# Fetching two weight matrices in turn, and a new order of the first units' decays, splits and masks, in a gated-attention and ELU-MLP kernel

## The chip, the cores and the metric

The kernel runs on one core of a Trainium2 chip. The metric is the device time of one execution in microseconds (us), lower is better. The work is done by five engines with queues of their own: TensorE (PE in the profile, PEld for its weight loads), VectorE (DVE), ScalarE (ACT), GpSimd (POOL) and SyncE (SP), which only issues DMAs here.

## The reference

Two stages follow each other. The first is a gated linear recurrence for 4 batches, 8 heads, 768 tokens and a head size of 48. The second is an MLP with an ELU, on 3072 tokens.

```python
f = 1.0 / (1.0 + np.exp(-f_logit))
for t in range(S):
    state = f[:, :, t, :, None] * state + np.einsum('bhd,bhe->bhde', k[:, :, t], v[:, :, t])
    y[:, :, t] = np.einsum('bhd,bhde->bhe', q[:, :, t], state)
x = y.transpose(0, 2, 1, 3).reshape(B * S, H * D)     # 3072 x 384
h = x @ w_in                                          # 384 x 2048
g = np.where(h > 0.0, h, np.exp(np.minimum(h, 0.0)) - 1.0)
out = g @ w_out                                       # 2048 x 384
```

q, k, v and f_logit are float32. The two weights arrive as float64, so that each is 6.3 MB.

## The kernel before

The function `fast` does the work (a second function, `general`, runs only when a check of the values fails, which it doesn't here). The tokens are cut into 12 units of 256. A unit's attention is worked out in chunks of 64 tokens and windows of 128. The decays are turned into running products: `gates` (ScalarE) makes 1 + exp(-f_logit), `grow` (VectorE, a scan) multiplies them up along the tokens, and `fall` (VectorE, a reciprocal) inverts the result. `scale` (GpSimd) multiplies k by the grown decays and q by the inverted ones. The 8 heads lie in 4 pairs (`HP`). The decays of pairs 0 to 2 (`NKT` = 3) are loaded; those of the last pair lie beside them in rows left over, and `move` brings them to their place by two DMAs, either for the grown decays (index 0), for the inverted ones (index 1), or for both.

After that, per unit: `transposed` turns k on TensorE into `psT`, and ScalarE copies it to `kn`; `advance` makes the chunks' contributions to the state (`psU_a`), `step` adds them up on VectorE; `scores` multiplies k and q (`psS`), `mask` puts the result into `at` on VectorE; `outputs` and `carried` (for unit 0: `first_outputs`) make `psY`, and ScalarE and VectorE copy it into `xt`, the input of the MLP.

The MLP takes the 2048 hidden columns in 8 steps of 256 (`NP`). `up` makes `psH` from `xt` and `wi`; `exped` (ScalarE) and `elu` (VectorE) make `gg`; `down` adds the product with `wo` to `psM`, two steps behind (`LAG`). Unit 0 does this with plain products (L949, L981). From unit 1 on, products of sums of blocks are used, with fewer of them (L904, L1015). They need sums of weights, which `mix` (GpSimd) and `combine` (VectorE) make once, and sums of inputs, which `blend` (GpSimd) makes of `xt`.

Weights come in 16 blocks of 768 KB, 8 of w_in and 8 of w_out, numbered in the order in which they are needed: w_in 0, 1, 2, w_out 0, w_in 3, w_out 1, and so on in turn. `fetch(n)` loads block n into slot n mod 7 of `area` (`AHEAD` = 7): a w_in block by one DMA of 576 KB (`MAIN`) and two of 96 KB (the rows of the last pair), a w_out block by one of 768 KB. The float64 words are made into float32 in three operations: `split(n)` takes the high words apart by two operations on VectorE (L568, L572), `lower(n)` brings the low words in on ScalarE (L578), and `merge(n)` adds both into `wi` or `wo` on VectorE (L586). `merge(n)` then calls `fetch(n + AHEAD)`, since its slot has come free.

The order of work on every engine is the order of the program's text (`manual_schedule`). Up to the first `up` the program is written out line by line. Behind it a loop runs over steps T, two for every step of the MLP: at even T `up`, at odd T `down`. `at_step(T, ...)` puts other work ahead of the step's own, and `later` puts a `split` and a `lower` behind it. The constants name steps: `A1` are the steps of unit 1's attention (transposes, both products, outputs, carried), `F1` the one at which unit 1's inverted decays are moved, `BL1` the one of its `blend`.

```python
    ...
    for n in range(1, NFT):
        t = min(max(needs[n][0] - 2, 0), n) + 2 * (n == NFT - 1)
        ...
    for T in range(NU * NFT):
        ...
        for f in plan.pop(T, ()):
            f()
        if T % 2 == 0:
            up(P)
        elif P >= LAG and T not in joint:
            ...
            down(P - LAG)
        for n in later.pop(T, ()):
            split(n)
            ...
```

`warm` issues products whose result nobody reads (`psW`): 128x512 ones, or, with `small`, 1x1 ones. They fill TensorE's time between the first products.

Of the kernel before, what the change touches and what calls it, by code (L numbers as in the profile page):

```python
# [9 lines left out]
I32 = mybir.dt.int32  # L10
# [346 lines left out]
def fast(ctx: ExitStack, tc: tile.TileContext, q, k, v, f_logit, w_in, w_out, out, flag, outer):  # L357
# [18 lines left out]
    nc = tc.nc  # L376
# [7 lines left out]
    NC = U // C  # L384
# [12 lines left out]
    WA = 1  # L397
    F1 = 3
    W0 = 3
    SMALL = 16  # L400
    MORE = 3
    RR = 2
    HOLD = 2
    A1 = (2, 8, 10, 11)
# [7 lines left out]
    BL1 = 13  # L412
# [58 lines left out]
    load(0, "fkq")  # L471
    load(1, "f")
    load(0, "v")
# [65 lines left out]
    def fetch(n):  # L539
        if n >= NFT:  # L540
            return
        j, out_ = parts[n]
        c = slice(j * 256, (j + 1) * 256)
        to = wo[:, 2 * j : 2 * j + 2] if out_ else wi[j][:]
        if wide:
            raws[n] = area[:, n % AHEAD]
            to = raws[n].rearrange("p (k f) -> p k f", k=to.shape[1])
        if out_:
            nc.sync.dma_start(out=to, in_=w_out[c, :].rearrange("(n p) f -> p n f", n=2))
            return  # L550
        nc.sync.dma_start(out=to[MAIN], in_=w_in[0 : NKT * 2 * D, c].rearrange("(k q) f -> q k f", k=NKT))
        rest = w_in[NKT * 2 * D :, c].rearrange("(r d k) f -> r d k f", r=2, d=PAD)
        for r in range(2):
            nc.sync.dma_start(out=to[GAP[r] : GAP[r] + PAD], in_=rest[r])

# [22 lines left out]
    def merge(n):  # L580
        if wide and n < NFT:
            hi = raws.pop(n).bitcast(I32)[:, 1::2]
            j, out_ = parts[n]
            to = wo[:, 2 * j : 2 * j + 2] if out_ else wi[j][:]
            bits, hi = (x.rearrange("p (k f) -> p k f", k=to.shape[1]) for x in (held.pop(n)[:], hi))
            nc.vector.tensor_tensor(out=to.bitcast(I32), in0=bits, in1=hi, op=ALU.add)  # L586
        fetch(n + AHEAD)
# [45 lines left out]
    def fall(u, p):  # L633

        f = qkf[u % NB]["f"]
        nc.vector.reciprocal(f[:, p, 1], f[:, p, 0])  # L636

    def move(u, which, queue):

        f = qkf[u % NB]["f"]  # L640
        for r in range(2):
            to = PAD + D * r
            queue.dma_start(out=f[to : to + D, NKT, which], in_=f[GAP[r] : GAP[r] + PAD, 0:NKT, which])

    def decays(u, p):
        grow(u, p)
        fall(u, p)
        scale(u, ("k", p, nc.gpsimd))
        if p:
            scale(u, ("q", p - 1, nc.gpsimd))  # L650
        if p == NKT - 1:
            move(u, slice(0, 2), nc.sync if u > 1 else nc.scalar)
# [415 lines left out]
    def warm(n, bank="m0", small=0):  # L1068

        pw = ps.tile([128, 4, 128], FP32, tag=bank, name="psW")  # L1070
        for _ in range(small):
            nc.tensor.matmul(pw[0:1, 0, 0:1], lhsT=ident[:, 0:1], rhs=ident[:, 0:1], start=True, stop=True)
        for _ in range(n):
            nc.tensor.matmul(
                pw[:], lhsT=ident[:], rhs=ident[:].unsqueeze(1).broadcast_to([128, 4, 128]), start=True, stop=True
            )


    gates(0, (1, 2))
    fetch(0)  # L1080
    load(1, "kqv")
    for n in range(1, HOLD):
        fetch(n)
    warm(W0, "m3")
    for p in range(NKT):
        grow(0, p)
        scale(0, ("k", p, nc.gpsimd))
        if p < 2:
            transposed(0, 0, "m0", (p,))
    move(0, 0, nc.scalar)  # L1090
# [3 lines left out]
    warm(WA, "m3")  # L1094
    gates(1, bias=0)
# [5 lines left out]
    )  # L1101
    fall(0, 1)
    scale(0, ("k", NKT, nc.gpsimd), ("q", 1, nc.gpsimd))
    fall(0, 2)
    move(0, 1, nc.scalar)
    warm(4)
    transposed(0, 1, "m1", (1,))
    advance(0, (2,))
    scores(0, None, (1,), pc)
    scale(0, ("q", 2, nc.gpsimd))  # L1110
    advance(0, (3,))
    scores(0, None, (2,), pc)
    nc.gpsimd.tensor_copy(
# [3 lines left out]
    a = qkf[1]["f"][:, 0:NKT, 0]  # L1117
    nc.vector.tensor_scalar_add(a, a, 1.0)
    for p in range(NKT):
        grow(1, p)  # L1120
    move(1, 0, nc.sync)
    scale(0, ("q", NKT, nc.gpsimd))
    warm(2)
    scores(0, None, (NKT,), pc)
    warm(1)
    fall(1, 0)
    split(0)
    for c in range(NC - 1):
        step(0, c)
    lower(0)  # L1130
    mask(0, pc)
    step(0, NC - 1)
    fall(1, 1)
    split(1)
# [5 lines left out]

    if wide:
        nc.gpsimd.memset(area[:, HOLD:].bitcast(I32)[:, :, 0:1], 0)
    for n in range(HOLD, AHEAD):
        fetch(n)
    merge(0)
    first_outputs(0)
    first_outputs(1)
    lower(1)
    scale(1, ("k", 0, nc.gpsimd), ("q", 0, nc.gpsimd), ("k", 1, nc.gpsimd), ("k", 2, nc.gpsimd))
    scale(1, ("k", NKT, nc.gpsimd))  # L1150
    fall(1, 2)
    watch(0)
    watch(1)
    scale(1, ("q", 1, nc.gpsimd), ("q", 2, nc.gpsimd))
    at_step(A1[2], lambda: outputs(1, ("m3", "m0")), lambda: lower(A1[2]), lambda: lower(A1[2] + 1))
    for n in range(1, NFT):
        t = min(max(needs[n][0] - 2, 0), n) + 2 * (n == NFT - 1)
        if t != A1[1]:
            at_step(t, lambda n=n: merge(n))
        if n > 1:  # L1160
            later.setdefault(max(min(t, n) - 2, 0), []).append(n)
    at_step(F1, lambda: move(1, 1, nc.scalar))
# [100 lines left out]
```

## Time and profile before

| | |
|---|---|
| time, median of 3 runs | 558.56 us (558.54 to 558.88) |
| profiled execution, its time | 559.46 us |
| profiled execution, its span | 557.7 us, mean granted TensorE clock 0.994 |
| busy: TensorE, VectorE, ScalarE, GpSimd | 543.0, 406.4, 228.3, 287.8 us |
| first `psH` of unit 0 (L949), of unit 1 (L904) | 30.28 us, 75.19 us |

The span runs from the first to the last instruction. The busy time of an engine is the time in which it executes, without waits. The page's slices are 40 equal parts of the span, here some 14 us each; a digit is the busy share in tenths. The chain that ended last goes back from the last instruction, at every step to what released it, or else to the instruction ahead of it in its engine's queue. An entry of the chain or of a timeline gives start, duration, engine, line and output; "x12" counts the machine's instructions, of which one float32 product makes two. All times of this text count from the start of the span, and durations are those of one profiled execution.

### The profile page before, as it was taken

The page shows a single profiled execution, that of the slowest core. Times are in us where ns is not written, and L with a number is a line of the kernel's source. Part 1 is how long each engine was busy: PE and PEld are TensorE (multiplying, and loading weights), DVE is VectorE, ACT ScalarE, POOL GpSimd, SP SyncE. Part 2 cuts the span into 40 slices and gives each one's busy share as a digit, 9 for nine tenths or more (in the row PEclk, how much of TensorE's full clock was granted, in tenths as well). Part 3 has the DMA queues.
Part 4 walks back from the last instruction along what each step waited for, and adds up shares of the span by engine and source line. Part 5 has one row for each costly group of instructions (what it writes and reads, how often), then busy time and mean ns, then how long its engine had stood idle before and what let it go on. Part 6 is the DMA issues. An engine that isn't in the chain of part 4 may idle for free.

```text
span 557.7 us, 15617 instructions
## 1 busy us (share of the span) xinstructions
PE 543.0 (97%) x6358; PEld 507.9 (91%) x6358; DVE 406.4 (73%) x804; ACT 228.3 (41%) x443; POOL 287.8 (52%) x559
## 2 busy tenths in 40 slices
PE   7889999999999999999999999999999999999996
PEld 3477679999999999999999999999999999999996
DVE  8799888887676776786785785786686687745553
ACT  3279764333434343333434334343343344333331
POOL 6600786475473474375465366357258258325332
PEclk9899999999999999999999999999999999999998
DMA  8998971033035135216217207307307302301001
GB/s 211 261 264 214 278 184 43 4 84 88 3 82 146 30 76 149 63 34 186 68 22 186 81 9 192 87 8 192 86 9 191 88 9 72 88 5 33 31 2 35
DMA packets 39474, 54.30 MB, mean 97 GB/s; under 512 B 4032, under 2 KB 29216, under 8 KB 39392
## 3 DMA queue, kind: packets, MB, share of 16 engines
q1 hardware_dynamic: 38592, 52.61, 36.5%
q8 instruction: 52, 0.85, 0.6%
q10 hardware_dynamic: 800, 0.59, 0.4%
q14 instruction: 30, 0.25, 0.2%
HBM read 45.02 MB, written 4.72 MB: 89 GB/s over the span
## 4 chain that ended last, share of the span: by engine, by line
PE 91%; DMA 2%; DVE 2%; ACT 1%; POOL 1%; issue 1%; SPq 1%; ACTq 0%; DVEq 0%; POOLq 0%
PE psH L904 39%; PE psM L1015 37%; PE psM L981 3%; PE psH L949 2%; PE psY L752 2%; PE psY L772 2%; PE psU_a L737 2%; PE psS L714 2%; PE psT L674 1%; DMA area<-in_moe_w_out_dram 1%; DMA f<-f 1%; ACT area L578 1%; DVE f L636 1%; POOL q L626 1%; DMA f<-in_f_logit_dram 0%
## 5 line engine op out<-in xcount | busy, mean ns | idle before, releaser
L904 PE MATMUL psH<-xt,wi 128*128 128x128 f32 (+1 forms) x1056 | 195.0, 294 | 0.0
L968 POOL TENSOR_TENSOR sums<-gg 128x128 f32<-128x128 f32 x172 | 75.6, 460 | 207.8 <-DVE gg L958 188.1
L936 ACT ACTIVATE gg<-hh 128x512 f32<-128x512 f32 x88 | 55.5, 630 | 249.3 <-DVE hh L926 111.7
L904 PEld LDWEIGHTS psH<-xt,wi 128*128 128x128 f32 x1056 | 149.5, 192 | 1.6
L904 PE MATMUL psH<-xt,area 128*128 128x128 f32 x704 | 121.5, 275 | 0.0
L904 PEld LDWEIGHTS psH<-xt,area 128*128 128x128 f32 x704 | 106.5, 192 | 4.5
L913 DVE TENSOR_TENSOR hh<-psH,u 128x256 f32<-128x256 f32 x88 | 36.9, 419 | 97.8 <-ACT u L911 97.7
L1015 PE MATMUL psM<-area,sums 128*128 128x192 f32 x516 | 99.9, 326 | 0.0
L1015 PEld LDWEIGHTS psM<-area,sums 128*128 128x128 f32 x516 | 86.0, 190 | 0.3 <-issue 0.2
L1015 PE MATMUL psM<-wo,gg 128*128 128x192 f32 x376 | 77.7, 332 | 0.0
L958 DVE SCALAR_TENSOR_TENSOR gg<-gg,hh 128x512 f32<-128x512 f32 x88 | 63.8, 725 | 1.5 <-ACT gg L937 1.5
L636 DVE RECIPROCAL f<-f 128x256 f32<-128x256 f32 x36 | 62.7, 1747 | 1.3
L937 ACT ACTIVATE gg<-gg 128x512 f32<-128x512 f32 x96 | 60.6, 631 | 3.0
L1015 PEld LDWEIGHTS psM<-wo,gg 128*128 128x128 f32 x376 | 60.2, 190 | 1.3
L926 DVE TENSOR_TENSOR hh<-psH,u43h 128x256 f32<-128x256 f32 (+1 forms) x176 | 54.6, 352 | 3.0
L626 POOL TENSOR_TENSOR q<-q,f 128x256 f32<-128x256 f32 x48 | 39.6, 826 | 19.5 <-DMA f<-f 12.9
L968 POOL TENSOR_TENSOR sums<-gg,sums 128x128 f32<-128x128 f32 x86 | 45.4, 528 | 6.7
L626 POOL TENSOR_TENSOR k<-k,f 128x256 f32<-128x256 f32 x48 | 39.3, 821 | 10.2 <-DMA f<-f 8.3
L926 DVE TENSOR_TENSOR u43h<-psH,hh 128x256 f32<-128x256 f32 x88 | 37.0, 420 | 9.2 <-PE psH L904 8.7
L968 POOL TENSOR_TENSOR sums<-sums,gg 128x128 f32<-128x128 f32 x86 | 43.0, 500 | 0.0
L1015 PE MATMUL psM<-area,gg 128*128 128x192 f32 x172 | 42.0, 326 | 0.0
L1015 PE MATMUL psM<-wo,sums 128*128 128x192 f32 x172 | 42.0, 326 | 0.0
(102 smaller groups left out, 646.3 us busy)
## 6 DMA issues: line engine op xcount, KB each, us to landing
area<-in_moe_w_out_dram SPq DMA_DIRECT2D x8, 768.0 KB, 10.6
again<-in_moe_w_in_dram SPq DMA_DIRECT2D x16, 384.0 KB, 3.6
again<-in_moe_w_out_dram SPq DMA_DIRECT2D x16, 384.0 KB, 3.6
k<-in_k_dram SPq DMA_DIRECT2D x12, 384.0 KB, 4.5
q<-in_q_dram SPq DMA_DIRECT2D x12, 384.0 KB, 5.6
v<-in_v_dram SPq DMA_DIRECT2D x12, 384.0 KB, 5.8
area<-in_moe_w_in_dram SPq DMA_DIRECT2D x8, 576.0 KB, 8.3
out_dram<-o SPq DMA_DIRECT2D x42, 96.0 KB, 2.4
```

The lines of the kernel that those rows point to most:

```text
L626: e.tensor_tensor(out=t[n][:, p], in0=t[n][:, p], in1=t["f"][:, p, "kq".index(n)], op=ALU.mult)
L636: nc.vector.reciprocal(f[:, p, 1], f[:, p, 0])
L714: nc.tensor.matmul(pc[r][FULL[b], w, p], lhsT=t["k"][FULL[r], p, cols], rhs=t["q"][FULL[r], p, cols], start=True, stop=True,)
L904: nc.tensor.matmul(to, lhsT=lhs, rhs=rhs, start=(n == 0), stop=True, skip_group_check=True)
L913: add = lambda to, x, y: nc.vector.tensor_tensor(out=to, in0=x, in1=y, op=ALU.add)
L926: add = lambda to, x, y: nc.vector.tensor_tensor(out=to, in0=x, in1=y, op=ALU.add)
L936: nc.scalar.activation(g[:], h, AF.Relu, scale=-1.0)
L937: nc.scalar.activation(g[:], g[:], AF.Exp, scale=-1.0)
L958: nc.vector.scalar_tensor_tensor(out=g[:], in0=g[:], scalar=-1.0, in1=phs.pop(P), op0=ALU.add, op1=ALU.max)
L968: nc.gpsimd.tensor_tensor(out=s[:, i], in0=x, in1=y, op=op)
L981: nc.tensor.matmul(pm[t][:], lhsT=g[:, i, t * 128 : (t + 1) * 128], rhs=wo[:, 2 * j + i, :], start=(j == 0 and i == 0), stop=(j == NP - 1 ...
L1015: nc.tensor.matmul(pm[bank][:, half * DH : (half + 1) * DH], lhsT=x, rhs=y, start=first, stop=(j == NP - 1), skip_group_check=True,)
```

## The change

- Loads of unit 0: v comes ahead of unit 1's f. The moved grown decays of unit 0 go by one DMA from ScalarE's queue and one from SP's, and SP issues `fetch(0)` and `fetch(1)` behind that one. Of unit 1 only k is loaded early; q and v come after blocks 6 and 7.
- `fetch` takes several blocks. With two, it issues their pieces in turn: a third of w_in's main rows, half of the w_out block, and so on, w_in's two small DMAs last. Blocks 2 and 3, 4 and 5, 6 and 7, up to 12 and 13 go like that. A list `after` and two `at_step` calls say when; the memset that held blocks 2 to 6 back is gone.
- The inverted decays of unit 0's last pair are made by a fourth reciprocal (`fall(0, NKT)`) and not by moving the others.
- Unit 1: `gates` adds its one on ScalarE and not on VectorE. Its scans come after `merge(0)`, its three reciprocals at steps 3, 4 and 5, the move of the inverted decays at step 6 (was 3), its transposes at step 7 (was 2).
- `mask` comes ahead of all but the first `step`; `split(2)` and `lower(2)` come ahead of the loop, `merge(2)` is at step 1, and blocks 3 and 4 are split a step earlier.
- Of the 11 long `warm` products 5 are left; 18 short ones come early, and at step 4 there are 5 short ones instead of 16. `BL1` is 12 instead of 13.

The core of the diff:

```diff
-    F1 = 3
-    W0 = 3
-    SMALL = 16
+    EARLY = 18
+    F1 = 6
+    W0 = 2
+    SMALL = 5
...
-    A1 = (2, 8, 10, 11)
+    A1 = (7, 8, 10, 11)
...
-    load(0, "fkq")
+    load(0, "fkqv")
     load(1, "f")
-    load(0, "v")
...
+    def fetch(*ns):
...
+            if out_:
+                rows = w_out[c, :].rearrange("(n p) f -> p n f", n=2)
+                pieces.append([(to[:, i], rows[:, i]) for i in range(2)] if len(ns) > 1 else [(to, rows)])
+                continue
+            main = w_in[0 : NKT * 2 * D, c].rearrange("(k q) f -> q k f", k=NKT)
+            rest = w_in[NKT * 2 * D :, c].rearrange("(r d k) f -> r d k f", r=2, d=PAD)
+            pieces.append(
+                ([(to[MAIN, k_], main[:, k_]) for k_ in range(NKT)] if len(ns) > 1 else [(to[MAIN], main)])
+                + [(to[GAP[r] : GAP[r] + PAD], rest[r]) for r in range(2)]
+            )
+        for i in range(max(map(len, pieces))):
+            for p in pieces:
+                if i < len(p):
+                    nc.sync.dma_start(out=p[i][0], in_=p[i][1])
...
-        fetch(n + AHEAD)
+        for what in after.get(n, ()):
+            fetch(*what)
...
-    move(0, 0, nc.scalar)
+    move(0, 0, (nc.scalar, nc.sync))
+    fetch(0)
+    fetch(1)
+    load(1, "k")
+    fetch(2, 3)
+    fetch(4, 5)
...
-    gates(1, bias=0)
+    gates(1)
...
-    fall(0, 2)
-    move(0, 1, nc.scalar)
-    warm(4)
...
+    fall(0, NKT)
+    scale(0, ("q", NKT, nc.gpsimd))
+    scores(0, None, (NKT,), pc)
...
-    a = qkf[1]["f"][:, 0:NKT, 0]
-    nc.vector.tensor_scalar_add(a, a, 1.0)
-    for p in range(NKT):
-        grow(1, p)
-    move(1, 0, nc.sync)
...
-    fall(1, 0)
     split(0)
-    for c in range(NC - 1):
-        step(0, c)
+    step(0, 0)
     lower(0)
     mask(0, pc)
-    step(0, NC - 1)
-    fall(1, 1)
-    split(1)
+    for c in range(1, NC):
+        step(0, c)
...
+    split(1)
+    after = {0: ((6, 7),), 6: ((12, 13),), 8: ((14,), (15,))}
     merge(0)
+    grow(1, 0)
     first_outputs(0)
     first_outputs(1)
     lower(1)
...
-    fall(1, 2)
+    split(2)
+    lower(2)
+    for p in range(1, NKT):
+        grow(1, p)
+    move(1, 0, (nc.sync, nc.sync))
+    load(1, "qv")
...
+    at_step(1, lambda: merge(2))
     at_step(A1[2], lambda: outputs(1, ("m3", "m0")), lambda: lower(A1[2]), lambda: lower(A1[2] + 1))
+    at_step(F1, lambda: move(1, 1, (nc.scalar, nc.scalar)), lambda: fetch(8, 9))
...
-        if n > 1:
-            later.setdefault(max(min(t, n) - 2, 0), []).append(n)
-    at_step(F1, lambda: move(1, 1, nc.scalar))
+        if n > 2:
+            later.setdefault(max(min(t, n) - 2 - (n < 5), 0), []).append(n)
+    for p in range(NKT):
+        at_step(F1 + p - NKT, lambda p=p: fall(1, p), lambda p=p: scale(1, ("q", p, nc.gpsimd)))
+    at_step(F1, lambda: fetch(10, 11))
```

## The prediction

> **What bounds the kernel now.** I read the page's busy shares and slices first, then the chain that ended last, then the timelines of ScalarE, VectorE and TensorE for the first 90 us, then the landing of each DMA there.
>
> ```profile
> span 557.7 us, 15617 instructions
> ...
> PE   7889999999999999999999999999999999999996
> ...
> PEclk9899999999999999999999999999999999999998
> DMA  8998971033035135216217207307307302301001
> ...
> PE 91%; DMA 2%; DVE 2%; ACT 1%; POOL 1%; issue 1%; SPq 1%; ACTq 0%; DVEq 0%; POOLq 0%
> ```
>
> TensorE holds 91% of the chain. Only the first three slices (14 us each) show it below nine tenths and the DMA engines full. The instruction orders of the two kernels differ only up to about 75 us; behind that TensorE runs one list without a wait, so what the change is worth is how much earlier or later the second unit's first `psH` starts (L904, 75.36 us).
>
> The chain of waits between 20 and 95 us:
>
> ```profile
> 29.67 0.55 DVE xt L829
> ...
> 30.26 1.75 DVE f L636
> ...
> 32.15 1.49 DVE wi L586
> ...
> 40.62 1.74 ACT area L578
> ...
> 42.38 0.97 DVE wi L586
> ...
> 43.48 2.83 PE psH L949 x12
> 46.31 2.58 PE psM L981 x8
> 48.89 1.08 PE psU_a L737 x64
> 49.97 0.95 PE psS L714 x64
> 50.91 2.79 PE psH L949 x12
> ```
>
> Up to 43.48 VectorE and ScalarE set the time (attention of unit 0 until `xt`, then the conversion of the float64 weights: `split` on VectorE, `lower` on ScalarE, `merge` on VectorE). From 43.48 on it is TensorE. The mark I use is the start of the fifth `psH` of unit 0 (call it H5), 50.91: everything that TensorE does between it and 75.36 has the same order in both kernels, 24.5 us, of which about 1 us is gaps.
>
> ScalarE's timeline shows why it matters where a copy stands in its queue:
>
> ```profile
> 38.18 1.18 ACT L678 COPY kn<-psT 128x512 f32<-128x512 f32 x2
> ...
> 45.06 3.92 ACT L578 ACTIVATE area<-area 128x768 uint16<-128x768 uint32 x2
> 48.71 0.69 ACT L936 ACTIVATE gg<-psH 128x512 f32<-128x512 f32 x1
> ```
>
> `kn`, which `psU_a` needs, is copied at 38.18, ten us ahead of need; the third and later `gg` wait behind two conversions each.
>
> [...] `gg` of the fourth `psH` (done at 46.3) starts at 48.71 behind `lower`. [...] Seen here once before the end: after the thin stretch 15.5 to 18.9 the granted clock is half for 3.41 us (mean by stretch: clock is the figure after POOL):
>
> ```profile
> 18.00:20.00 2.00, 1.68 (x56) 1.44 (x50) 1.89 (x4) 1.09 (x3) 2.00 (x3) 0.73 1.07 282
> 20.00:22.00 2.00, 2.00 (x3) 0.75 (x3) 0.00 (x0) 1.27 (x1) 2.00 (x7) 0.50 1.03 195
> ```
>
> [...] a `split` takes 1.01+0.97 beside GpSimd work and 0.56+0.56 without.
>
> **The change, part by part.**
>
> *Front, unit 0.* The inverse of the last decays, `fall(0, NKT)`, replaces two DMAs that carried it (issued 13.33 and 13.93, landed 17.88 and 19.29). It costs a fourth reciprocal: three end at 13.29, plus 1.65 gives 14.95. It needs the moved decays; these were issued at 10.15 behind ScalarE's copies and behind 0.8 MB of weights, and landed at 16.35. Now one goes to ScalarE, one to SP, at 8.5 (the scans end at 8.43), with only unit loads in flight (the five end at 11.06): landed about 11.5, hidden. The price: `fetch(0)` and `fetch(1)` queue behind it on SP. `fetch(0)` is issued at 9.1 to 10.8 instead of 6.2 to 10.0, but starts when the loads drain, 11.1, and takes 3.4 as before: 14.5 (before 14.46). Free, as `split(0)` wants it at 14.95. Then `split(0)` with GpSimd active 1.95: 16.9; the last `psS` is ready at about 16.4. `mask` starts at 16.9 where it was 23.43. From mask to the first `psH` the same operations follow (30.28 − 23.43 = 6.85; the state steps after the masks, 1.45, and `merge(0)` fit beside `psY`). First `psH` about 23.8 instead of 30.28: 6.5 us earlier. Floor, with a 1.1 `split`: 23.0. Ceiling: six fewer long warming products (11 become 5; short ones fill in) leave TensorE thin up to 18; if the clock is then half under `psY` (2.2 + 1.7 us, and short products took 0.70 for 0.46 in that state), add up to 2: 25.8. The two scale edits cancel: +0.85 on ScalarE and −0.62 on VectorE, neither path waited for. Masks ahead of steps are in the 6.85. The removed GpSimd memset (0.1) freed `fetch(2)` from waiting until 20.9.
>
> *Transfers.* In pieces, a pair of blocks is seven DMAs instead of four: 3 issues more, about 1.4 us of SP per pair, under the transfer. Before, a pair took 6.0 to 6.2 us (landings 30.76, 36.98, 43.13). [...] I take 6.0, the low end is 4.6 (1.57 MB at the best mixed slice, 339 GB/s), and nothing slower than 6.2 is shown. `fetch(1)` lands at 18.0, the second unit's k at 19.4, so the pair 2,3 at 25.2 (24.0 if fast) with w_in's last piece at its end. After 4,5 (31) and 6,7 (37) come the moved decays, q and v of unit 1 (3 us), and 8,9 at 46.
>
> *The conversion after it.* Call T0 the start of `split(2)`: max of the `xt` copy's end, 23.8, and the landing, 25.2. I take 25.0. What VectorE then does in a fixed order up to the end of `split(7)`: six splits at 1.07, five merges (1 to 5) at 0.98, two scans 1.2, watches 0.15, two `elu` at 0.6, and the **three inverses of unit 1 that are now here** (before at 15.65, 25.30, 30.26) at 1.67. Sum 6.4 + 4.9 + 1.35 + 1.2 + 5.0 = 18.9. ScalarE's inputs are ready in time, so it ends at T0 + 18.9 = 43.9. Five us of it are the moved inverses: they give back most of the 6.5 us.
>
> *The new wait.* `A1[0]` goes from 2 to 7, so the transposes of unit 1 stand behind the fourth `psH`, and ScalarE copies `kn` behind `lower(7)`, `gg` of that product and `lower(8)`. From 43.9: 0.1 + 1.83 + 1.26 + 1.88 + 0.6 (first half of `kn`) = 49.5, where `psU_a` can start. It started at 48.89 before. Queued behind the waiting `psU_a` on TensorE: `psS`, H5 and all later. TensorE's `psM` before it needs `merge(5)`, T0 + 16.1, and is done at T0 + 18.8 = 43.8: it idles 5.7 us. The two DMAs of `move(1, 1)`, now at step 6, issue while `lower(7)` runs, and land about 5 us later (5.3 and 4.9 before): 49 to 50, then 0.7 on GpSimd for q: in time for the last `psS`. A second way gives the same: blocks 8,9 land at 46, `split(8)` 1.07, `lower(8)` 1.88, `kn` 0.6: 49.5. Then `psU_a` and `psS`, with the tail of the copy, 2.1: H5 at 51.6 to 51.7, 0.8 later than before. VectorE's slower mode beside the eight scalings of unit 1 on GpSimd (5.8 us, before mostly ahead of the first `psH`) adds 0 to 2, I take 0.5. The idle stretch of 5.7 us is longer than the thin one that halved the clock before: 3.41 us at half speed lose between 0.7 (short products) and 1.7 (long ones); I take 1.3. Of the 1 us of gaps after H5, 0.2 may be regained.
>
> *No cost.* The blend one step earlier waits for `xt` and precedes one `mix`; TensorE reaches 75 later than it is ready. Eleven short products fewer at step 4 fall in idle time.
>
> Sum: 0.8 + 0.5 + 1.3 − 0.2 = **+2.4 us**. The profiled execution took 559.46 for its span of 557.7; the median is 558.56, 0.9 lower. The span should be near 560.1, the median 558.56 + 2.4 = 561.0.
>
> **Rivals.** *The early start wins* (0.25). T0 = 23.0 (short `split(0)`, quick pair, clock full) gives `split(7)` 41.9, H5 at 49.7, −1.2, and 0.8 of the later gaps regained: 556.5. It decides if T0 falls below 24.2, without a loss of clock. For: the front loses DMA round trips that lie on the chain (5.44 us for f alone). Against: the 18.9 us of VectorE cannot shrink. If, against my reading, `kn` doesn't hold TensorE up, H5 comes at 45.9 and 555 is open.
>
> *Even* (0.13). T0 = 24.3 and a full clock: H5 at 51.0, 558.6.
>
> *Worse* (a quarter of the slower cases). Clock half under `psY` too, T0 = 26.5: +1.5 on the sum, 562.5[...].
>
> *Fetching in turn does nothing.* It is in the sum already; if it helps, T0 falls by 1.0 and no more.
>
> **How the numbers follow.** Slower 0.62 (own range 559.7 to 564), even 0.13, faster 0.25. A measurement of this kernel can tell about 0.2%, 1.1 us, from no change. 80% range 556.0 to 564.0: it leaves out the faster cases beyond the walk's floor and the double loss of clock.
>
> **What would show it.** Right: first `psH` near 24, `split(7)` near 44, TensorE idle some 5 us before `psU_a` of unit 1 with ScalarE's `kn` copy as releaser, and a half clock near 50. Wrong: `psU_a` before 48, or the fifth `psH` before 50. If the pairs land every 5 us or less, the price of the transfers was wrong.

## The result, and the profile after

The changed kernel takes 567.09 us (median of 4 runs, 566.08 to 567.81), the kernel before 558.55 us (557.92 to 558.88). The ratio is 1.0153, with a 95% interval of 1.0135 to 1.0171: slower, as forecast, but by 8.5 us where 2.4 were forecast, and above the upper end of the range.

The page of the changed kernel, the lines that answer to those shown of before:

```profile
span 565.4 us, 15635 instructions
...
PE   6776999999999999999999999999999999999996
...
PEclk8979999999999999999999999999999999999999
DMA  7998972005006207307307207307306302201001
...
PE 89%; DVE 4%; DMA 4%; issue 1%; ACT 1%; POOL 1%; SPq 1%; ACTq 0%; DVEq 0%; POOLq 0%
```

The fourth slice (42 to 57 us) of TensorE has lost its 9, and the chain now has 4% of DMA and 4% of VectorE in place of 2% each. Everything lies ahead of 125 us again: behind it the products of the changed kernel run 7.7 us behind those of the kernel before, up to the end.

The chain of waits of the changed kernel (start, duration, engine, what):

```profile
12.09 7.75 DMA area<-in_moe_w_in_dram
...
20.46 7.78 DMA area<-in_moe_w_in_dram
...
28.33 0.57 DVE bits L571
...
37.47 1.66 DVE f L640
...
41.92 1.66 DVE f L640
...
45.87 1.66 DVE f L640
```

From 12.09 to 28.33 it is a chain of transfers, then of VectorE, with the three moved inverses (`f`, L640) in it. The timeline of VectorE has the wait itself:

```profile
28.33 0.56 DVE L571 TENSOR_SCALAR bits<-area 128x768 int32<-128x768 int32 x1 [3.42 <-DMA area<-in_moe_w_in_dram]
```

`split(2)`, T0 of the prediction, starts at 28.33 and not at 25.0: its block had landed at 28.25. What follows is the queue that was foreseen. The timelines of ScalarE and of TensorE:

```profile
48.97 1.92 ACT L581 ACTIVATE area<-area 128x768 uint16<-128x768 uint32 x1 [2.00 <-DVE area L575]
...
50.64 0.68 ACT L940 ACTIVATE gg<-psH 128x512 f32<-128x512 f32 x1
51.35 0.63 ACT L941 ACTIVATE gg<-gg 128x512 f32<-128x512 f32 x1
51.89 1.91 ACT L581 ACTIVATE area<-area 128x768 uint16<-128x768 uint32 x1
53.54 1.16 ACT L682 COPY kn<-psT 128x512 f32<-128x512 f32 x2
```

```profile
54.27 0.31 PE L741 MATMUL psU_a<-v,kn 64*64 64x48 f32 x2 [4.28 <-ACT kn L682]
54.75 1.59 PE L741 MATMUL psU_a<-v,kn 64*64 64x48 f32 x59 [0.16 <-ACT kn L682]
...
56.18 2.00 PE L718 MATMUL psS<-q,k 64*64 64x64 f32 x63
58.11 3.04 PE L953 MATMUL psH<-xt,wi 128*128 128x256 f32 x12
```

`lower(7)`, `gg`, `lower(8)`, then `kn`: TensorE idles 4.28 us, runs the next products at half clock (the granted clock is 0.50 from 55.11 to 58.52), and the fifth `psH` (H5) comes at 58.11 in place of 50.84. In this trace that is the whole loss. But taking it away alone gains nothing, as the runs below show: a second limit of the same height stands behind it. The stretches of time (the last three figures are granted clock, DMA share, GB/s) show the DMA engines nearly idle in the same place, and SyncE's own waits from 44 to 65 us say why (who waited, for what; us in total, how often, the longest):

```profile
48.00:50.00 2.00, 2.00 (x7) 0.85 (x5) 2.00 (x3) 1.03 (x1) 0.52 (x1) 1.00 0.11 38
50.00:52.00 2.00, 0.00 (x0) 0.00 (x0) 1.93 (x4) 1.97 (x4) 0.07 (x1) 1.00 0.56 98
```

```profile
SPq L560 <- DVE wi L589: 4.1, 1, 4.1
```

In step 6 of the program `merge(6)` comes ahead of `fetch(10, 11)`, and `merge(6)` issues blocks 12 and 13. SyncE's order is therefore 8 and 9, **12 and 13, 10 and 11**. Block 13 goes into the slot that `merge(6)` frees at 50.40; SyncE waits for that with the first piece of block 13, and blocks 10 and 11, whose slots have been free since `merge(4)` (41.92), stand behind it. Their last piece lands at 65.06. VectorE waits for it:

```profile
65.14 0.56 DVE L571 TENSOR_SCALAR bits<-area 128x768 int32<-128x768 int32 x1 [2.73 <-DMA area<-in_moe_w_in_dram]
```

`merge(9)`, queued behind that `split(10)`, ends at 67.16. TensorE comes to the product that needs it at 68.63, so this wait isn't seen in TensorE: it is 1.5 us short of being the bound itself.

### The profile page after: what moved, and what is told of

It is laid out like the page before. It is cut to its first block, busy times and chain, and to the rows that moved or that the text cites. A ratio compares the mean times of both kernels' runs of the same rounds, so it can differ in the third digit from the quotient of the medians.

```text
span 565.4 us, 15635 instructions
## 1 busy us (share of the span) xinstructions
PE 542.5 (96%) x6360; PEld 509.4 (90%) x6360; DVE 408.0 (72%) x804; ACT 229.9 (41%) x444; POOL 290.6 (51%) x558
## 4 chain that ended last, share of the span: by engine, by line
PE 89%; DVE 4%; DMA 4%; issue 1%; ACT 1%; POOL 1%; SPq 1%; ACTq 0%; DVEq 0%; POOLq 0%
PE psH L908 38%; PE psM L1019 36%; PE psM L985 3%; DMA area<-in_moe_w_in_dram 3%; PE psU_a L741 2%; PE psY L776 2%; PE psY L756 2%; PE psS L718 2%; PE psH L953 2%; PE psT L678 1%; DVE f L640 1%; DMA k<-in_k_dram 1%; SPq L560 1%; DVE bits L571 0%; DVE wi L589 0%
## 5 line engine op out<-in xcount | busy, mean ns | idle before, releaser
L908 PE MATMUL psH<-xt,wi 128*128 128x128 f32 (+1 forms) x1056 | 195.0, 294 | 0.0
L908 PEld LDWEIGHTS psH<-xt,wi 128*128 128x128 f32 x1056 | 149.5, 192 | 1.6
L908 PE MATMUL psH<-xt,area 128*128 128x128 f32 x704 | 121.8, 275 | 0.3 <-DVE hh L930 0.3
L908 PEld LDWEIGHTS psH<-xt,area 128*128 128x128 f32 x704 | 106.5, 191 | 5.2 <-PE psH L908 0.5
L640 DVE RECIPROCAL f<-f 128x256 f32<-128x256 f32 x37 | 64.4, 1746 | 1.2
L630 POOL TENSOR_TENSOR k<-k,f 128x256 f32<-128x256 f32 x48 | 40.6, 848 | 22.8 <-DVE f L635 11.3
```

The costliest lines, as they stand in the source:

```text
L630: e.tensor_tensor(out=t[n][:, p], in0=t[n][:, p], in1=t["f"][:, p, "kq".index(n)], op=ALU.mult)
L908: nc.tensor.matmul(to, lhsT=lhs, rhs=rhs, start=(n == 0), stop=True, skip_group_check=True)
```

## The experiments

Each was timed beside runs of the kernel before on the same chip; the ratio is to those (their medians were 558.8 to 559.9). Times of events are from each kernel's profiled execution, in us. That one took up to 3.7 us more than the median (e15, 567.49) and up to 1.5 less (e3, 561.61), so a row's events need not add up to its median. "psU_a" is its first product in unit 1. A star marks a `split(10)` before which VectorE waits for a DMA; without one, the block had landed when VectorE came to it.

| | median us | ratio to before (95%) | first psH | split(2) | psU_a | H5 | split(10) |
|---|---|---|---|---|---|---|---|
| before | 558.55 | | 30.28 | 33.56 | 48.82 | 50.84 | 56.34 |
| after | 567.09 | 1.0153 (1.0135 to 1.0171) | 25.87 | 28.33 | 54.27 | 58.11 | 65.14* |
| e1_one_by_one | 566.01 | 1.0104 (1.0072 to 1.0136) | 30.44 | 27.50 | 56.05 | 60.14 | 64.37 |
| e2_kn_step5 | 567.89 | 1.0137 (1.0106 to 1.0169) | 27.32 | 27.85 | 49.89 | 52.76 | 65.44* |
| e3_kn_and_move_step5 | 563.10 | 1.0057 (1.0039 to 1.0076) | 25.82 | 27.64 | 49.31 | 51.34 | 57.56 |
| e4_inverses_early | 566.48 | 1.0121 (1.0090 to 1.0151) | 26.78 | 29.07 | 51.98 | 56.08 | 63.45* |
| e5_warm | 566.61 | 1.0143 (1.0103 to 1.0183) | 26.25 | 27.64 | 53.46 | 55.95 | 64.31* |
| e6_fetch_first | 568.60 | 1.0187 (1.0142 to 1.0233) | 28.02 | 27.54 | 54.10 | 58.20 | 65.43* |
| e7_order | 567.34 | 1.0149 (1.0107 to 1.0191) | 26.08 | 28.48 | 54.50 | 58.44 | 62.67 |
| e8_order_kn5 | 564.56 | 1.0087 (1.0049 to 1.0125) | 27.70 | 28.70 | 49.69 | 55.08 | 59.32 |
| e9_step5_inverses | 562.88 | 1.0062 (1.0039 to 1.0084) | 26.63 | 30.02 | 49.37 | 51.40 | 59.01 |
| e11_step5_inv_blend13 | 563.03 | 1.0064 (1.0042 to 1.0087) | 27.10 | 29.73 | 49.20 | 51.23 | 60.26* |
| e13_step5_inv_warm0 | 563.86 | 1.0079 (1.0055 to 1.0102) | 32.18 | 29.94 | 49.62 | 51.65 | 59.44 |
| e12_before_in_turn | 560.93 | 1.0036 (1.0020 to 1.0051) | 29.09 | 32.37 | 48.91 | 50.93 | 58.12 |
| e14_step5_single | 562.46 | 1.0063 (1.0046 to 1.0080) | 27.74 | 25.12 | 51.37 | 53.39 | 57.63 |
| e15_step5_single_inv | 563.83 | 1.0081 (1.0052 to 1.0111) | 28.29 | 30.12 | 56.07 | 58.09 | 62.33 |
| e16_single | 566.15 | 1.0117 (1.0097 to 1.0138) | 29.95 | 27.15 | 55.11 | 59.20 | 63.43 |
| e17_order_move_last | 566.43 | 1.0141 (1.0119 to 1.0162) | 26.04 | 27.51 | 53.19 | 57.28 | 61.51 |
| e18_before_front | 559.00 | 0.9999 (0.9983 to 1.0015) | 28.54 | 31.82 | 48.19 | 50.21 | 56.16 |
| e19_before_front_warm | 558.75 | 0.9997 (0.9985 to 1.0008) | 30.17 | 33.45 | 48.72 | 50.74 | 56.23 |

### The first four: the pairs, kn's place, the inverses

The theory at this point was kn's queue alone, with the late landing of block 2 and the half clock as rivals.

**e1_one_by_one**, the same order of blocks, but block by block:

```diff
-    fetch(2, 3)
-    fetch(4, 5)
+    for n in range(2, 6):
+        fetch(n)
...
-    after = {0: ((6, 7),), 6: ((12, 13),), 8: ((14,), (15,))}
+    after = {0: ((6,), (7,)), 6: ((12,), (13,)), 8: ((14,), (15,))}
...
-    at_step(F1, ..., lambda: fetch(8, 9))
+    at_step(F1, ..., lambda: (fetch(8), fetch(9)))
...
-    at_step(F1, lambda: fetch(10, 11))
+    at_step(F1, lambda: (fetch(10), fetch(11)))
```

> The changed kernel (567.1 us) with one edit: every pair of blocks is fetched one block after the other, not piece by piece in turn. Theory 'queue' (VectorE's fixed order from split(2) on, then the kn copy behind lower(8) on ScalarE, set the start of the fifth psH of unit 0, 58.2): block 2 no longer shares the engines with block 3 and lands at 22.0 + 3.4 = 25.5 instead of 28.25, split(2) starts 2.8 us earlier and everything behind it too: 564.3. Theory 'landing' (the arrival of every block sets the pace): block 8 too comes 2.7 us earlier, 564.3, but block 3 lands no earlier than now. Theory 'turn is free' (only the sum of a pair's bytes counts): 567. Theory 'clock' (the half clock of TensorE costs most): 567.

566.01. Block 2 landed at 25.46 and not at 28.25, so the pairs do hold up the first block of each; but in this execution (568.09, the slowest of its runs) the clock was half from 10.02 to 20.25, the first `psH` came only at 30.44, and TensorE waited 5.51 us for `kn`. `split(10)`, at 64.37, came behind the masks of unit 1, which wait for `psS`, and not behind its block. The interval just touches that of the changed kernel: inconclusive on the pairs.

**e2_kn_step5**:

```diff
-    A1 = (7, 8, 10, 11)
+    A1 = (5, 8, 10, 11)
```

> The changed kernel with the transposes of unit 1 and the kn copies at step 5 instead of 7; the move of the inverted decays stays at step 6. 'Queue': kn is copied behind lower(6), near 47 to 48, so psU_a starts right behind the second psM at 50 instead of 54.3; the last psS waits for the moved decays (landed 51.9) until 53: fifth psH at 53.5 to 54, 4 us earlier than now, 562 to 563. 'Landing': the sixth psH needs block 8, landed 49.1 and merged not before 54 to 55, it can't profit by more than 3 us: 564. 'Clock': the idle stretch ahead of psU_a goes and with it the half clock, 565 from that alone.

567.89, no gain. The idle time before `psU_a` is gone, H5 is at 52.76, 0.7 us ahead of the forecast (51.65, and 0.5 and 1.3 for GpSimd and the clock), and nothing of it arrives. TensorE's timeline shows where it went:

```profile
49.89 1.15 PE L741 MATMUL psU_a<-v,kn 64*64 64x48 f32 x64
52.36 0.46 PE L718 MATMUL psS<-q,k 64*64 64x64 f32 x16 [0.61 <-POOL q L630]
67.52 5.49 PE L985 MATMUL psM<-wo,gg 128*128 128x384 f32 x8 [4.35 <-DVE wo L589]
```

and VectorE's, what that `wo` waited for:

```profile
65.44 0.56 DVE L571 TENSOR_SCALAR bits<-area 128x768 int32<-128x768 int32 x1 [7.41 <-DMA area<-in_moe_w_in_dram]
66.03 0.56 DVE L575 TENSOR_SCALAR area<-area 128x768 int32<-128x768 int32 x1
66.51 0.95 DVE L589 CUSTOM_DVE_ANT_0 wo<-area,bits 128x1536 uint16<-128x1536 uint16 x1
```

The wait has moved 13 us on (its end from 54.27 to 67.52): it now hangs on block 10, which the order of the fetches holds up. The eight products behind the idle stretch, at half clock, take 5.49 us for 2.74. The queue theory alone falls with this run.

**e3_kn_and_move_step5**, `A1[0]` = 5 and `F1` = 5:

```diff
-    F1 = 6
+    F1 = 5
...
-    A1 = (7, 8, 10, 11)
+    A1 = (5, 8, 10, 11)
```

> As the run before, and the move of the inverted decays at step 5 too (with the three inverses at steps 2, 3 and 4). 'Queue': neither kn nor the last psS is late, fifth psH near 52 to 53: 561 to 562. If the second wait (the moved decays) didn't matter, the same time as the run before.

563.10, 5 us less than e2. `F1` is also the step of `fetch(8, 9)` and `fetch(10, 11)`; at step 5 they come ahead of `merge(6)`, and `split(10)` starts at 57.56. This run changed two things beside kn, the move and the order; e7 and e8 take them apart.

**e4_inverses_early**, unit 1's scans and two inverses where VectorE waits for block 2:

```diff
-    split(2)
-    lower(2)
     for p in range(1, NKT):
         grow(1, p)
+    for p in range(2):
+        fall(1, p)
+    split(2)
+    lower(2)
...
     for p in range(NKT):
-        at_step(F1 + p - NKT, lambda p=p: fall(1, p), lambda p=p: scale(1, ("q", p, nc.gpsimd)))
+        if p == 2:
+            at_step(F1 + p - NKT, lambda p=p: fall(1, p))
+        at_step(F1 + p - NKT, lambda p=p: scale(1, ("q", p, nc.gpsimd)))
```

> The changed kernel with unit 1's scans and its first two inverses ahead of split(2), where VectorE waits for block 2 from 24.9 to 28.3; the third inverse stays at step 5. 'Queue': VectorE's chain up to split(7) gets 1.2 + 3.3 us shorter and starts 1.3 us later (29.6), so split(7) ends near 45.7 instead of 48.95 and all behind comes 3.2 us earlier: 564. 'Landing': block 8 lands at 49.1 as now, lower(8) can start at 50.2 at the earliest instead of 51.9: 1.7 us, 565.4.

566.48. `psU_a` comes 2.3 us earlier, H5 2.0, the first `psH` of unit 1 (L908) 1.1 (80.59). `split(10)` still waits, until 63.45, but here TensorE has no wait between H5 and L908. What is lost on the way is the clock, half until 58.45 and so over most of H5 (2.97 in the changed kernel's chain):

```profile
56.15 3.94 PE psH L953 x12
```

### The second four: the order alone, the front, the clock

**e7_order**:

```diff
-    at_step(F1, ..., lambda: fetch(8, 9))
+    at_step(F1, ..., lambda: fetch(8, 9), lambda: fetch(10, 11))
...
-    at_step(F1, lambda: fetch(10, 11))
```

> Only the order in which SyncE issues three pairs changes: blocks 10 and 11 are fetched directly behind 8 and 9, ahead of 12 and 13 (in the changed kernel merge(6) comes first in step 6 and issues 12 and 13, whose second slot comes free only at 50.40 us, with 10 and 11 queued behind). Theory of two limits, one behind the other (kn's place in ScalarE's queue, then the late landing of 10 and 11): kn alone still holds psU_a, which starts at 54 as before, split(10) starts near 58 instead of 65.14, the DMA engines aren't idle from 46 to 50; time 566 to 567, almost no gain. Theory that the order alone is the loss: 561 to 562.

567.34: mending the order alone gives nothing either, as the theory of two limits had it. TensorE waits 5.41 us for `kn`. `split(10)` came at 62.67 and not near 58, but not for its block, which had landed at 58.16. VectorE reaches it only behind the masks, which wait for `psS` and so for `kn`:

```profile
58.55 1.29 DVE L726 TENSOR_TENSOR at<-psS,twice 128x512 f32<-128x512 f32 x2 [3.67 <-PE psS L718]
```

The block would have landed earlier still: SyncE's waits show that another one had taken the place of the wait for `merge(6)`.


```profile
SPq L560 <- DMA f<-f: 4.5, 1, 4.5
```

A piece of block 11, with the rest of block 10 behind it, waits for the move of the inverted decays, which ScalarE issues only at 49.26, in its own queue. The traces have a reason: the DMAs of the program, on whichever queue, count up eight semaphores (the "lanes" of later texts), and none was issued before the one that had its semaphore last had landed (no exception among 260 in e7's trace, 260 in that of the changed kernel, 244 in that of the kernel before). The piece (issued 52.63) and the move (landed 52.62) have the same one. The kernel before has such a wait too, of 5.8 us, with the DMA share at 0.36 from 44 to 48 us; there block 9, issued at 45.42, has the semaphore of the move that landed at 45.37:

```profile
SPq L549 <- DMA f<-f: 5.8, 1, 5.8
```

**e8_order_kn5**, the edit of e7 and of e2, the move left at step 6:

```diff
-    A1 = (7, 8, 10, 11)
+    A1 = (5, 8, 10, 11)
...
-    at_step(F1, ..., lambda: fetch(8, 9))
+    at_step(F1, ..., lambda: fetch(8, 9), lambda: fetch(10, 11))
...
-    at_step(F1, lambda: fetch(10, 11))
```

"The third run" in this text and in later ones is e3, "the fourth" e4.

> The order of e7 and unit 1's transposes at step 5, with the move of the inverted decays left at step 6. Two limits: psU_a near 50 as with the transposes alone, and psM at L985 doesn't wait 4.35 us near 63 us, nor run at half clock after it (another 2.7 us): 560.5 to 562. If the move of the decays at step 5 was what brought the gain of the third run, and not the order: 566 to 568, as with the transposes alone.

564.56. With kn and the order mended, the loss falls from 1.5% to 0.9%, where each alone gave nothing: the two limits stood one behind the other. It stops short of the forecast, since the moved decays land at 51.91 and 53.71 among the weights, and `psS` waits for `q`:

```profile
54.69 0.46 PE L718 MATMUL psS<-q,k 64*64 64x64 f32 x16 [3.14 <-POOL q L630]
```

**e6_fetch_first**, blocks 0 and 1 ahead of the first move, which goes to ScalarE's queue whole:

```diff
+    fetch(0)
+    fetch(1)
     warm(W0, "m3", EARLY)
...
-    move(0, 0, (nc.scalar, nc.sync))
-    fetch(0)
-    fetch(1)
+    move(0, 0, (nc.scalar, nc.scalar))
```

> Blocks 0 and 1 are issued by SyncE ahead of the moved decays of unit 0, both of which go to ScalarE's queue. Theory that the weights queue behind the move and that the DMA engines have a hole there (share 0.73 from 10 to 12 us): split(0) no longer waits for its last 96 KB piece, split(2) starts at 26 instead of 28.33, first psH near 25; but unit 0's decays may land later (13 instead of 11.6) behind 1.5 MB of weights, which delays the fourth inverse and the first masks. With the late landing of blocks 10 and 11 still there, at most 1 of 2.4 us reaches the end: 565.5 to 567. If the front sets the end: 564.5.

568.60. Block 0 landed at 15.61 instead of 16.92, but the moved decays at 15.09 instead of 11.61, and the first `psH` came at 28.02. For the first `psH` the order that the change chose was the better one; the times don't tell the two apart (the intervals overlap).

**e5_warm**, four long warming products each at steps 2 and 8:

```diff
+    at_step(2, lambda: warm(4, "m3"))
     at_step(4, lambda: warm(0, "m3", SMALL))
+    at_step(8, lambda: warm(4, "m3"))
```

> Four long warming products more at step 2 and four at step 8, in the two stretches of 4.2 us in which TensorE waits. Theory that the half clock costs 1.8 us at psU_a and psS: clock full from 31 to 38 and from 55 to 58, psU_a and psS in 2.1 instead of 3.9, fifth psH at 56.4, time 565 to 566. Theory that blocks 10 and 11, landing at 65.06, stand right behind: the fifth psH comes earlier but psM near 66 to 68 waits for merge(9) instead, time 566.5 to 567. Products that take longer than the idle stretch would add: 568.

```profile
53.94 1.08 PE L741 MATMUL psU_a<-v,kn 64*64 64x48 f32 x59 [0.16 <-ACT kn L682]
...
54.88 1.15 PE L718 MATMUL psS<-q,k 64*64 64x64 f32 x63
55.95 2.86 PE L953 MATMUL psH<-xt,wi 128*128 128x256 f32 x12
```

The clock stays full (1.08 for 1.59, 1.15 for 2.00), H5 comes 2.2 us earlier, and the time is 566.61, inside the interval of the changed kernel. The loss of clock was real. Of the 2.2 us 0.9 are left at the first L908 (80.78), since the second limit now shows: the chain to L908 runs through the last piece of blocks 10 and 11 (57.97 to 64.24).

### The third four: what is left

**e9_step5_inverses** is e3 and e4 together (both diffs above):

> The third and the fourth run's edits together: transposes and move at step 5 (which also puts blocks 10 and 11 ahead of 12 and 13), and unit 1's other scans and two of its inverses ahead of split(2), where VectorE waits for transfers. Theory that the chain of VectorE from split(2) on is the next limit: the fourth psH near 40.6 instead of 42.69, the fifth near 49.3 instead of 51.34, first L908 near 73, time 2 less than the third run: 561. Theory that a later stretch (unit 2's decays and the sums of weights on VectorE and GpSimd, 80 to 117 us) takes the gain back: fifth psH near 49.3, time 562.5 to 563.5.

**e11_step5_inv_blend13** starts from e9:

```diff
-    BL1 = 12
+    BL1 = 13
```

> As the run before this one in the list, with the blend of unit 1 at step 13 as it was before the change. If the blend's earlier place on GpSimd is what loses the 1.7 us between 80 and 117 us, this run is 1 to 1.7 us below that one; if not, the same within 0.5 or slower by up to 1.

**e13_step5_inv_warm0** too:

```diff
+    at_step(0, lambda: warm(6, "m3"))
```

> As the first run of this list, with six long warming products ahead of the first psH, where TensorE waits some 2.7 us for xt. Clock full in the first psH (2.8 us instead of 4.5): if TensorE is behind VectorE only there, up to 1.7 us less; if VectorE's conversion sets the fourth psH, no change within 0.5.

562.88, 563.03 and 563.86, all like e3. The earlier inverses push `split(2)` back to 30.02, so that the fourth `psH` came at 44.11 and not at 40.6. Moving the blend back changed nothing that can be measured. The warming products of e13 started late, took 5.42 us, and put the first `psH` off to 32.18; the clock was full (the mean of its span is 1.000), H5 at 51.65. In e9 TensorE waits for `wo` at 67.2 (1.17 us) and 74.2 (0.36): the late blocks again.

**e12_before_in_turn** is the kernel before with the new `fetch`, its pairs, and nothing else:

```diff
-    for n in range(HOLD, AHEAD):
-        fetch(n)
+    fetch(2, 3)
+    fetch(4, 5)
+    after = {0: ((6, 7),), 2: ((8, 9),), 4: ((10, 11),), 6: ((12, 13),), 7: ((14,),), 8: ((15,),)}
```

> The kernel before with nothing but the fetching in turn: pairs 2 and 3, 4 and 5 where blocks 2 to 6 were issued, 6 and 7 after merge(0), 8 and 9 after merge(2), 10 and 11 after merge(4), 12 and 13 after merge(6). Block 2 arrives with block 3, some 3 us later than before, so split(2) starts at 31 instead of 33.56 or the same, as VectorE is late anyway. Theory that the fetching in turn itself costs little: 558.5 to 560. Theory that the pairs arrive too late for the splits (both blocks of a pair at once, and each pair only when both slots are free): 561 to 563.

560.93, ratio 1.0036 (1.0020 to 1.0051): fetching in turn costs by itself some 2 us. `split(2)` is no later (32.37). `split(8)` and `split(12)`, which wait for nothing in the kernel before (48.50 and 61.73), now wait for their blocks:

```profile
50.27 0.56 DVE L573 TENSOR_SCALAR bits<-area 128x768 int32<-128x768 int32 x1 [1.13 <-DMA area<-in_moe_w_in_dram]
...
64.16 0.56 DVE L573 TENSOR_SCALAR bits<-area 128x768 int32<-128x768 int32 x1 [1.12 <-DMA area<-in_moe_w_in_dram]
```

A pair waits for both its slots, and the first of its blocks for the second, which would make them late; no run separates this from the smaller pieces.

### The last six: single blocks, the lane, the front alone

**e14_step5_single** is e3 with single blocks, block n + 7 behind `merge(n)`; **e15_step5_single_inv** adds e4's edit; **e16_single** has the single blocks without e3's edits:

```diff
-    fetch(2, 3)
-    fetch(4, 5)
+    for n in range(2, 6):
+        fetch(n)
...
-    after = {0: ((6, 7),), 6: ((12, 13),), 8: ((14,), (15,))}
+    after = {n: ((n + AHEAD,),) for n in range(1, 9)}
+    after[0] = ((6,), (7,))
...
-    at_step(F1, lambda: move(1, 1, ...), lambda: fetch(8, 9))
+    at_step(F1, lambda: move(1, 1, ...))
...
-    at_step(F1, lambda: fetch(10, 11))
```

> Transposes and move at step 5 as in the third run, and the weights no longer in pairs: every block by whole DMAs, block n + 7 issued behind merge(n), as in the kernel before. In the runs so far SyncE's issue of a weight piece waits 4.0 to 4.5 us for a DMA of ScalarE's (the move of the decays) to land, whose completion lane the piece is to use again; a pair in turn takes seven of the eight lanes, two single blocks take four. Theory that the transfers in pairs are what is left: no such wait, DMA engines full from 40 to 56, the last w_in pair landed near 62 instead of 65, first L908 near 74, time 559.5 to 561. Theory that VectorE's later stretch holds the end anyway: 562 to 563.

> As the run before, with two inverses and the scans of unit 1 ahead of split(2). If VectorE's chain is the limit once the transfers aren't: 1 to 2 below the run before, 558 to 559.5. If transfers still are: the same.

> The changed kernel with the weights block by block (n + 7 behind merge(n)), transposes still at step 7. kn still holds psU_a, to 53 or 54, so the fifth psH stays near 57 to 58: 565 to 567. If the pairs alone were the loss: 561.

562.46, 563.83 and 566.15. e16 is still held by kn (`psU_a` at 55.11). In e14 `split(2)` starts 2.5 us earlier than in e3, and TensorE then waits in its transposes for k scaled by unit 1's moved grown decays, in e15 for 5.72 us (in an execution 3.7 us above the median):

```profile
41.55 0.44 PE L678 MATMUL psT<-ident,k 128*128 128x128 f32 x2 [2.92 <-POOL k L630]
```

These decays land at 40.27 and 40.61 in e14, behind blocks 2 to 7. The kernel before had issued them ahead of block 2, and they landed at 24.26. That is a fourth limit. SyncE's wait for ScalarE's move, which was expected to go, grew to 8.8 us in e14.

**e17_order_move_last** puts the move behind both fetches in e7's text:

```diff
-    at_step(F1, lambda: move(1, 1, ...), lambda: fetch(8, 9), lambda: fetch(10, 11))
+    at_step(F1, lambda: fetch(8, 9), lambda: fetch(10, 11), lambda: move(1, 1, ...))
```

> Blocks 10 and 11 ahead of 12 and 13 as in e7_order, and the move of the inverted decays behind both fetches in the program's text. Every engine's own list is the same as in that run; only which completion lane a DMA gets is different. If SyncE's wait of 4.5 us there is for the lane: it goes, blocks 10 and 11 land near 54 instead of 58, and the move on ScalarE waits instead. Time as there, 566 to 568, as kn holds psU_a. If SyncE's wait has another cause, it stays.

566.43, and the wait stays at 4.0 us. The semaphores turned out to be dealt as in e7, so the run changed nothing: it doesn't test the shared semaphore. That cause rests on the landings and issues that coincide, not on a run that takes it away.

**e18_before_front** is the kernel before with the fourth inverse and the early first move:

```diff
-    move(0, 0, nc.scalar)
+    move(0, 0, (nc.scalar, nc.sync))
+    fetch(0)
+    load(1, "kqv")
...
-    move(0, 1, nc.scalar)
+    fall(0, NKT)
...
-    fall(1, 0)
     split(0)
...
     step(0, NC - 1)
+    fall(1, 0)
     fall(1, 1)
```

> The kernel before with one thing of the change: the fourth inverse of unit 0 in place of the second move, and the first move issued ahead of the weights by two queues; unit 1's first inverse goes behind unit 0's masks. Transfers in single blocks, unit 1's transposes, its moves and its other inverses stay as before. Theory that the front's gain is real and only the rest of the change spent it: first masks near 20.5 instead of 23.43, first psH near 27.3 instead of 30.28, split(7) done 1 to 2 us earlier, as far as the blocks' landings (43.13 for block 7) let it: 556.5 to 558 beside 559. Theory that the landings of blocks 2 to 8 set the time anyway: 558.5 to 560, same as before.

**e19_before_front_warm** adds to that:

```diff
+    at_step(0, lambda: warm(3, "a0"))
```

> As e18_before_front, with three long warming products in the 3.24 us in which TensorE waits for the first xt. In that run the first psH took 4.46 us at half clock, and ScalarE, idle for 4.56 us, waits for it and then has no gap up to kn: gg, two conversions, kn. Theory that this chain (first psH, ScalarE) is now the limit: first psH 2.8 us, ScalarE some 1.2 us earlier (its conversions then wait for the splits), fifth psH near 49.2, time 557 to 558, about 1 below both that run and the kernel before. Theory that the landings of blocks 4 to 8 hold it: psU_a near 48 as there, 558.5 to 559.5.

559.00 and 558.75: the same as the kernel before, within 0.17%. In e18 the masks begin at 19.87 and H5 comes 0.6 us earlier. In e19 the first `psH` runs at full clock (2.86 for 4.46), but starts at 30.17, after a half clock from 10.08 to 13.49; its chain up to the weights of the fourth `psH` (43.38) is made of transfers:

```profile
23.16 9.84 DMA area<-in_moe_w_in_dram
...
33.01 6.87 DMA area<-in_moe_w_in_dram
...
40.54 1.71 ACT area L578
```

So in e19 transfers hold the fourth `psH`: an earlier front would find the blocks not yet there. In e18 it is different: `split(2)` (31.82) waits for no block, and the chain runs through the first `psH` at half clock and then through ScalarE. None of these runs is faster than the kernel before.

## Why the prediction was right or wrong

**Right.** The direction, and the mechanism that it named: `kn` behind `lower(7)`, `gg` and `lower(8)`, TensorE idle before `psU_a` with ScalarE's copy as releaser, the half clock after it. From the end of `split(7)` (48.94) to the first `psU_a` (54.27) it took 5.3 us, forecast 5.6, and from there to H5 3.8, forecast 3.4 (2.1 and 1.3 for the clock). The moved decays of unit 0 landed at 11.41 and 11.61, forecast 11.5. The first three pairs took 6.2, 6.1 and 5.3 us, forecast 6.0.

**Wrong in the sum for H5**, +7.3 and not +2.6 (0.8 + 0.5 + 1.3). Two terms, T0 (3.3 us later than forecast) and VectorE's list (1.7 us longer, of which 0.5 were allowed for), make up nearly all of that.
- T0 was 28.33, not 25.0. The step that failed is "`fetch(0)` takes 3.4 as before: 14.5". Its last piece, issued at 10.82 to 11.41, landed at 16.92, 2.4 us late, with `fetch(1)` on its heels; the DMA share from 10 to 12 us was 0.73. `fetch(1)` (20.21 for 18.0), k (22.05 for 19.4) and the pair (28.25 for 25.2) came later by 2.2, 2.7 and 3.1 us, so most of the delay arose here. How much of it the order of issue made isn't shown: e6, with blocks 0 and 1 issued first, had block 0 1.3 us earlier and `split(2)` 0.8.
- VectorE's list took 20.6 us, not 18.9. It was busy for 20.30 of them. The splits cost 7.5 and not 6.4 (those of blocks 6 and 7 about 1.5 each: their second operation took 0.98 and 0.96 beside GpSimd's scaling of q, 0.56 in the four others), and the stretch of the two watches with the wait behind them 1.2 and not 0.15. The 0.5 for GpSimd was too little for the first.

**Wrong in its frame.** The step was "everything that TensorE does between it and 75.36 has the same order in both kernels", from which H5 alone was to tell the result. The order was the same; the blocks that this work needs were not there. The prediction followed the transfers up to 8 and 9 (46 forecast, 49.10 measured) and stopped. e2 shows what that missed: with H5 at 52.76 TensorE waits 4.35 us for a weight at 63, and the kernel still takes 567.89. So even the forecast H5 would have met such a wait. In the changed kernel itself this limit costs nothing yet, as it ends 1.5 us ahead of the other. Taking away either gives nothing (e2, e7); both give 0.66% by the difference of the ratios, 3.7 us (e8), and with the move early as well 0.96%, 5.4 us (e3).

**The rival "Fetching in turn does nothing"** was wrong: e12 gives it 2 us of loss by itself. Of the pairs I had costed the three more issues, and not that a pair waits for two slots.

**The rival "worse"** had both terms in the right direction: T0 = 26.5 gave it 562.5, and the upper 2 us for VectorE beside GpSimd 564. The first was less than half of T0's delay (1.5 of 3.3), the second about what VectorE's list took more (1.7), though not for GpSimd alone.

**The front.** The first `psH` came at 25.87 and not at 23.8, at my ceiling. The rival that the early start wins is answered in part by e18: with the fourth inverse and the early move alone the ratio is 0.9999 (0.9983 to 1.0015). But its first `psH` is 1.7 us earlier (28.54) and not 4.4 as in the changed kernel, so a whole front without the losses stays untested.

**The end.** From H5 to the first L908 it regained 0.8 us (0.2 forecast), then lost 1.2 by 125 us, where VectorE's `hh` is late for one `psH` (0.33 us seen as a wait). With the 7.3 of H5 that makes the 7.7 us by which the two profiled spans differ. e3, which reaches L908 at 75.09 against 75.19, is 1.7 us behind by 113. e12, with nothing but the pairs, loses 1.0 us in the same stretch, and e14, without them, 0.9, so the pairs alone don't explain it; e11 excludes the blend's step. The cause stays open, and so does how e3's remaining 3 us divide between this stretch and the pairs.

## What to carry to other kernels

Follow every queue, the DMA queue too, past the point that you expect to be the bound: list the transfers in the order of issue, with the slot that each waits for, and see what stands behind the one that waits. When one repair gives nothing, look for the wait that took its place before giving up the theory, and test the two together. An earlier start is worth only what the next resource on the path can take.

## What was not expected of the hardware

- A DMA was held up by a DMA of another engine's queue. In e7 SyncE, with its slot free, waited 4.5 us for ScalarE's 48 KB move, and the same wait stands in the kernel before (5.8 us). By the traces it comes from the semaphores that this program deals out, and no run takes it away.
- Splitting the transfers brought no gain: the first two pairs in seven pieces take 6.2 and 6.1 us, as two pairs in four pieces did; only the third took 5.3. The DMA share is 0.96 from 28 to 49 us of the changed kernel, and e12 is slower by 0.36%.
- But for the last 3 us, the half clock came in stretches of 3.41 us or multiples of it, at other places in each of four executions (18.93 to 22.35 in the kernel before; 10.73 to 14.15, 31.21 to 38.04 and 55.11 to 58.52 in the changed kernel; 10.02 to 20.25 in e1; none before 562 us but 9.55 to 12.97 and 26.62 to 30.04 in e5). In the trace of the changed kernel the clock changes at 10.73 and, for the last time, at 563.69 us, 162 steps of 3.413 us apart, with all the other changes on the same grid, and the grid lies elsewhere in each of the four. A first `psH` that falls into such a stretch took up to 1.7 us longer (4.46 in e18, for 2.8).
